# Gate transfer placed behind the convolution, the stage matrix and output weights let in one at a time by GpSimd fills, three x pieces ahead of q's weights, and a new order of the work

## The chip, the core and the metric

The kernel runs on one core of one Trainium2 chip. The metric is the device time in microseconds (us) of one execution; the times below are of separate executions, and the profile is of one more. The engines are TensorE (PE, with its weight loads as PEld), VectorE (DVE), ScalarE (ACT), GpSimd (POOL) and SyncE (SP), each of which works through its own list of instructions in the order written; DMA transfers are issued by SP, POOL and ACT.

## What is computed

From x (2048 x 640), k, v and some weights the kernel makes two results and mixes them row by row:

```
g = sigmoid((x * gate_w).sum(-1))
kv = (4-tap causal filter of k along the rows, per channel) * v
a = x * (fft-convolution of kv with ssm_k along 2048 rows, per channel, + kv * ssm_D)
q, k, v = x @ wqkv, 32 heads of 20; each row attends to rows s, s-2, ..., s-14
b = softmax(q k / sqrt(20)) v, all heads, @ wo
out = g * a + (1 - g) * b
```

## The kernel before

A planner (class `Plan`) runs at build time. The parts of the work are generators (`loads`, `xpose`, `vproj`, `qkproj`, `fragger`, `score_gen`, `pv_gen`, `conv`, `gate`, `h_stream`, ...), each of which asks for one engine at a time with an estimated cost; the planner picks the request whose estimated start plus 120 ns times its priority (table `PRI`) is least, and the instructions are written to the engines' lists in that order. `LEAN_QK`, `LEAN_V` and `LEAN_H` tilt the choice between ACT and DVE for copies out of PSUM; `BG` and `pipe` tell how far the estimated DMA pipe has to be drained before a paced load asks for its fill. The lists are fixed when the kernel runs.

The work in order of time:

- **Projections.** x comes in eight pieces of 256 rows (`xn`). TensorE turns each over (`tx`, 10 transposes a piece), and DVE copies it to `xT`. `psv` (18 units of 10 matmuls, line 528) is the projection to v for one block of 121 rows; it needs the weights `Wv`, which lie in the tile `KX`. `pj` (30 units of 10 matmuls, line 575) is the projection to q and k: for each fifth `ft` of the features first three units of q, then three of k, with the weights `Wqk` (loads W0 for q, W1 for k). Each unit is copied by ACT or DVE to `stg`, of which there are two, one for q and one for k; a new `stg` can be written only when the transfers out of the old one have landed.
- **Fragments.** GpSimd sends the rows of `stg` on to `qb` and `kb` in transfers of up to 20 rows (`fragger`, line 614), three sets of each in turn. Set `t` holds heads 4t to 4t+3.
- **Attention**, for t = 0 to 7: `sc` (line 636) are the scores, ACT takes the exponential (line 643, ten instructions a t), `O` (line 664) is their product with v, and DVE divides (`rd`, `oS`, lines 673 and 676). The four PSUM tiles `ps0` to `ps3` are shared by all stages.
- **Filter of k ("the convolution")** on DVE: 24 multiplications and 18 additions (lines 481 and 488) inside `KX`, from row 64 down, and at the end four products with v (line 492, into `vin`). It starts when the last k load has landed.
- **Gate.** 20 matmuls (`gps`, line 542), an exponential by ACT to `grow`, the first 1024 columns of `KX`, four small DMA transfers on SP's queue from there to `g_nat` (line 551), and three small DVE instructions (lines 554 to 556). The transfers read single rows at a wide stride, and a DVE instruction that writes elsewhere in `KX` behind them waits until they have landed; the transfers in turn wait for the DVE instructions on `KX` ahead of them.
- **Transform** of ssm_k (key h) and kv (key u), each in two halves P of 40 channel groups: per half ten units `s1` (line 697) and eleven `s2` (line 713), each of which ACT or DVE copies out of PSUM. `s2` needs the stage matrix G, four loads into `SX`, which takes the place of `KX`. `Hw` is a copy of the h result with its halves swapped, made by four transfers for each P (lines 805 and 807). 44 products on DVE (line 751), the output projection `op` (line 854, 16 units), the inverse (`i`, lines 820 and 893) and the mix (lines 901 to 908) end the kernel.

SP issues nearly all loads, in the order written. `load` only issues. `paced` first lets GpSimd fill one column of the target, and the load waits for that fill, so that its place in GpSimd's list tells when the load may start. Before, v (8 loads) and ssm_k (16 loads, `h_lin`) are paced.

Of the kernel before, what the change touches and what calls it, by code (L numbers as in the profile page):

```python
# [18 lines left out]
D = 640  # L19
# [26 lines left out]
QC = 160  # L46
CR = 11
WARM = 8
BG = 1491.0


def _np_bf16(a):
# [78 lines left out]
class Req:  # L131


    def __init__(self, engs, cost=0.0, deps=(), take=0, give=(), n=0, move=0.0, pri=None, mode=None, bg=None, mm=0, lean=0.0):
# [3 lines left out]

LAT = {("P", "A"): 230.0, ("P", "D"): 230.0, ("A", "P"): 120.0, ("D", "P"): 120.0, ("A", "D"): 100.0, ("D", "A"): 100.0}
SWITCH = 110.0  # L140
LEAN_QK = -187.0
LEAN_V = -490.0
LEAN_H = 56.0
PRI = dict(loads=0, fragger=0, xpose=-6.6, score_gen=-9.9, pv_gen=-6.9, conv=-3.3, conv_v=-2.7, bulk=0, conv_end=0, qkproj=-6.1, vproj=-6.6,
           gate=-16.1, load_G=0, h_slot=0, p2_slot=41.0, u_slot=0, swaps=0, load_T=0, op_tr=24.4, outproj=37.1, load_q=0, products=28.7, final=-12.8,
           h_stream=(-6.1, 2.1), u_stream=(1.4, 19.9), inverse1=(31.7, 33.5))
PAGE = 256
FETCH = 3600.0

# [1 line left out]
class Plan:  # L151


    def __init__(self, nslots):
        self.at = dict(P=0.0, A=0.0, D=0.0, G=0.0, S=0.0, Q=0.0)
        self.mode = None
        self.count = 0
        self.page = 0.0
        self.pipe = 0.0
        self.row = 0.0  # L160
        lane = []
        self.lane = {"S": lane, "Q": lane, "G": []}
        self.slots = [Bank() for _ in range(nslots)]
        self.streams = []
        self.log = []
# [91 lines left out]
def kernel(  # L257
# [14 lines left out]
    nc = tc.nc  # L272
# [3 lines left out]
    cf = {k: nc.inline_tensor(v, name=f"cf_{k}") for k, v in fft_consts().items()}  # L276
# [32 lines left out]
    Wv, kin, pab, wraw, wl = [KX[:, e - n:e] for e, n in zip(ends, sizes)]  # L309
    grow = KX[:, 0:1024].bitcast(F32)  # L310
    Wv = Wv.rearrange("p (t n) -> p t n", t=NDT)
# [24 lines left out]
    W3 = B_wqkv.rearrange("(t p) (w n) -> p t w n", p=128, w=3)  # L336
# [3 lines left out]
    def ev(name):  # L340
        if name not in E:
            E[name] = Ev()
        return E[name]
# [10 lines left out]
    def load(name, dst, src, us, deps=()):  # L354
        g = yield Req("S", 650.0, deps, move=us)
        nc.sync.dma_start(dst, src)
        mark(name, g)

    def paced(name, dst, src, us):
        g = yield Req("G", 200.0, bg=BG, pri=2)  # L360
        nc.gpsimd.memset(dst[:, 0, 0:1], 0.0)
        yield from load(name, dst, src, us, [g.done])

    def load_x(a):
        yield from load(f"x{a}", xn[:, a], raw(x2, 256 * a * D, [[2 * D, 128], [D, 2], [1, D]]), 1250.0)

    def loads():
        yield from load_x(0)
        yield from load("Wv0", Wv[:, 0:3], W3[:, 0:3, 2, :], 1700.0)
        yield from load_x(1)  # L370
        yield from load("W0", Wqk[:, :, 0, :], W3[:, :, 0, :], 2800.0)
        yield from load_x(2)
        yield from load_x(3)
        yield from load("W1", Wqk[:, :, 1, :], W3[:, :, 1, :], 2800.0)
        for a in range(4, 8):
            yield from load_x(a)
        for c in (1, 0):
            for q in range(4):
                yield from load(f"k{q}{c}", kin[32 * q:32 * q + 32, 3 + 32 * c:35 + 32 * c, :],
                                raw(k2, 32 * c * D + QC * q, [[64 * D, 32], [D, 32], [1, QC]]), 2000.0)  # L380
        for c in range(2):
            for q in range(4):
                yield from paced(f"v{q}{c}", vin[32 * q:32 * q + 32, c], raw(v2, QC * q + 80 * c, [[64 * D, 32], [D, 64], [1, 80]]), 2100.0)
        yield Req("S", 1.0, [ev("xtr")])
        h_lin = p0.tile([128, 80, 2, 64], BF, name="h_lin", tag="HL")
        st["h_lin"] = h_lin
        for P in range(2):
            for q in range(4):
                for c in range(2):
                    yield from paced(f"h{P}{q}{c}", h_lin[32 * q:32 * q + 32, PL * P:PL * P + PL, c, :],  # L390
                                     raw(A_ssm_k, (160 * q + 80 * c + PL * P) * S, [[64, 32], [S, PL], [1, 64]]), 1200.0)
# [12 lines left out]
    def load_G():  # L404
        yield Req("S", 1.0, [ev("conv"), ev("grow"), ev("vproj")])
        SX = p0.tile([128, 10240 + 8192], BF, name="SX", tag="KX")
        st["SX"] = SX
        st[("h", 0)] = SX[:, 0:10240].rearrange("p (c o m l) -> p c o m l", c=2, o=10, m=128)
        G = SX[:, 10240:].rearrange("p (a r b) -> p a r b", a=32, r=2)
        st["G"] = G  # L410
        at("SX", 0.0)
        for a in range(4):
            yield from load(f"G{a}", G[:, 8 * a:8 * a + 8], cf["G"].ap().rearrange("p (a r b) -> p a r b", a=32, r=2)[:, 8 * a:8 * a + 8], 1700.0)

    def load_T():
        yield Req("S", 1.0, [ev("p2")])
        wo = st["p2"].tile([128, NDT, D], BF, name="wo")
        st["wo"] = wo
        yield from load("wo", wo[:], B_wo.rearrange("(t p) n -> p t n", p=128), 2700.0)
        yield Req("S", 1.0, [ev("hw1")])  # L420
        T = st["p2"].tile([128, 64, 2, 32], BF, name="T")
        st["T"] = T
        yield from load("T", st["T"][:], cf["T"].ap().rearrange("p (a r b) -> p a r b", a=64, r=2), 2700.0)
# [112 lines left out]
    def gate():  # L536
        g = yield Req("P", 1300.0, [ev("xtr"), ev("vproj")] + xdeps(0, HS), take=1, mode="g", mm=20)
        gps = psum(g, "gps", (128, 512))
        for dt in range(NDT):
            for c in range(4):  # L540
                o = X0 + HP * (c // 2) + 512 * (c % 2)
                nc.tensor.matmul(gps[32 * c:32 * c + 32, :], lhsT=wgz[:, dt, :], rhs=xT[:, dt, o:o + 512],
                                 start=(dt == 0), stop=(dt == NDT - 1), tile_position=(0, 32 * c), skip_group_check=True)
        mark("gatePE", g)
        r = yield Req("A", 600.0, [g.done], give=g.banks)
        nc.scalar.activation(grow, gps[:], ACT.Exp, scale=-1.0)
        src = grow[0:1, 0:1]
        pt = src.ap[0][0]
        for gg in range(4):
            r = yield Req("S", 500.0, [r.done] if gg == 0 else [], move=200.0)  # L550
            nc.sync.dma_start(g_nat[32 * gg:32 * gg + 32, :], raw(src, 64 * (gg % 2) * pt + 16 * (gg // 2), [[32 * pt, 2], [32, 16], [1, 16]]))
        mark("grow", r)
        r = yield Req("D", 500.0, [Ev(r.done.t + 8000.0)])
        nc.vector.tensor_scalar(g_nat[:], g_nat[:], 1.0, None, ALU.add)
        nc.vector.reciprocal(g_nat[:], g_nat[:])
        nc.vector.tensor_scalar(omg[:], g_nat[:], -1.0, 1.0, ALU.mult, ALU.add)
        mark("gate", r)
# [357 lines left out]
    for gen in (loads, fragger, xpose, score_gen, pv_gen, conv, bulk, conv_v, conv_end, qkproj, vproj, gate, load_G, h_slot, p2_slot,  # L915
                u_slot, swaps, load_T, op_tr, outproj, load_q, products, final):
        plan.add(gen(), PRI[gen.__name__])
    for gen in (h_stream, u_stream, inverse1):
# [33 lines left out]
```

## Time and profile before

| | |
|---|---|
| median of 3 executions | 257.19 us (256.75 to 258.81) |
| profiled execution: time | 257.08 us |
| profiled execution: span | 255.3 us |
| granted TensorE clock, mean | 0.889 of full speed |
| busy: PE, DVE, ACT, POOL | 216.6, 185.5, 168.7, 69.2 us |
| DMA moved | 33.82 MB in 59579 packets, 49212 of them under 512 B |

The span is the time from the first to the last record of the profile, and 1.8 us of the execution lie outside it. No engine is busy all the time, so what bounds the kernel changes from stage to stage, and the views below are read by stage.

### The profile page before, as it was taken

The page shows a single profiled execution, that of the slowest core. Times are in us where ns is not written, and L with a number is a line of the kernel's source. Part 1 is how long each engine was busy: PE and PEld are TensorE (multiplying, and loading weights), DVE is VectorE, ACT ScalarE, POOL GpSimd, SP SyncE. Part 2 cuts the span into 40 slices and gives each one's busy share as a digit, 9 for nine tenths or more (in the row PEclk, how much of TensorE's full clock was granted, in tenths as well). Part 3 has the DMA queues.
Part 4 walks back from the last instruction along what each step waited for, and adds up shares of the span by engine and source line. Part 5 has one row for each costly group of instructions (what it writes and reads, how often), then busy time and mean ns, then how long its engine had stood idle before and what let it go on. Part 6 is the DMA issues. An engine that isn't in the chain of part 4 may idle for free.

```text
span 255.3 us, 8331 instructions
## 1 busy us (share of the span) xinstructions
PE 216.6 (85%) x3648; PEld 168.6 (66%) x3654; DVE 185.5 (73%) x221; ACT 168.7 (66%) x221; POOL 69.2 (27%) x142
## 2 busy tenths in 40 slices
PE   7799999990799799979859898899999999994590
PEld 3699888860456556746636687688887798884350
DVE  1224799942887978979848879989999998053851
ACT  2143455590348857658948969989986589767971
POOL 6698897220153635438500000000000000000000
PEclk9999999996599979999655569989999999999568
DMA  6999958992789888932992002960089992400663
GB/s 231 303 336 183 183 76 151 146 152 31 120 114 161 130 138 140 137 80 52 256 239 90 1 5 53 229 135 3 3 173 218 193 232 78 103 3 5 157 158 103
DMA packets 59579, 33.82 MB, mean 133 GB/s; under 512 B 49212, under 2 KB 56008, under 8 KB 58904
## 3 DMA queue, kind: packets, MB, share of 16 engines
q1 hardware_dynamic: 55192, 27.08, 53.6%
q0 software_dynamic: 3792, 5.81, 11.4%
q8 instruction: 28, 0.46, 0.8%
q10 hardware_dynamic: 560, 0.42, 0.5%
q14 instruction: 7, 0.06, 0.1%
HBM read 20.01 MB, written 2.62 MB: 89 GB/s over the span
## 4 chain that ended last, share of the span: by engine, by line
PE 50%; DVE 17%; DMA 11%; ACT 8%; issue 8%; POOL 2%; SPq 1%; DVEq 0%; POOLq 0%; ACTq 0%
PE psv L528 10%; PE op L854 10%; PE pj L575 9%; DMA kb<-stg 7%; PE i L820 7%; DVE Hs L286 5%; PE s L713 3%; DVE stg L286 3%; ACT ETall L643 3%; PE sc L636 3%; DMA xn<-in_A_q_dram 3%; ACT UC L284 2%; PE O L664 2%; PE tx L467 2%; ACT yb L901 2%
## 5 line engine op out<-in xcount | busy, mean ns | idle before, releaser
L643 ACT ACTIVATE ETall<-sc 121x912 bf16<-121x912 f32 (+1 forms) x80 | 63.4, 856 | 26.1 <-PE sc L636 25.6
L575 PE MATMUL pj<-xT,Wqk 128*128 128x342 bf16 (+1 forms) x300 | 51.5, 322 | 0.4 <-ACT ETall L643 0.4
L575 PEld LDWEIGHTS <-Wqk 128*128 128x128 bf16 x300 | 28.8, 100 | 16.1 <-issue 0.7
L636 PE MATMUL sc<-qb,kb 31*128 31x114 bf16 x576 | 22.5, 239 | 16.1 <-DVE stg L286 8.0
L284 ACT CAST UC<-s 128x960 bf16<-128x960 f32 (+2 forms) x32 | 29.4, 992 | 2.2 <-PE s L713 1.8
L636 PEld LDWEIGHTS <-kb 31*128 31x128 bf16 x576 | 13.4, 103 | 25.9 <-issue 17.4
L481 DVE TENSOR_TENSOR KX<-KX 128x1760 bf16<-128x1760 bf16 (+1 forms) x24 | 27.7, 1162 | 3.0 <-DMA g_nat<-KX 1.7
L614 POOL DMA_DIRECT2D qb<-stg x36 | 18.1, 505 | 39.9 <-PE sc L636 25.6
L528 PE MATMUL psv<-KX,xT 128*121 128x320 bf16 x180 | 28.0, 306 | 0.0
L854 PE MATMUL op<-wo,oT 128*128 128x128 bf16 (+1 forms) x154 | 24.9, 317 | 0.7 <-issue 0.2
L284 ACT CAST VW<-psv 121x640 bf16<-121x640 f32 x16 | 11.1, 695 | 21.0 <-PE psv L528 21.0
L528 PEld LDWEIGHTS <-xT 128*121 128x121 bf16 x180 | 24.2, 138 | 1.1
L488 DVE TENSOR_TENSOR KX<-KX 128x1760 bf16<-128x1760 bf16 (+1 forms) x18 | 18.8, 1042 | 7.2 <-DMA g_nat<-KX 6.9
L713 PEld LDWEIGHTS <-SX 64*128 64x128 bf16 x512 | 19.9, 98 | 3.5 <-issue 2.5
L854 PEld LDWEIGHTS <-oT 128*128 128x128 bf16 x160 | 17.1, 149 | 7.6 <-issue 2.3
L614 POOL DMA_DIRECT2D kb<-stg x36 | 17.9, 503 | 10.1 <-ACT stg L284 6.7
L284 ACT CAST stg<-pj 128x684 bf16<-128x684 f32 (+1 forms) x14 | 10.4, 743 | 14.9 <-PE pj L575 11.3
L286 DVE COPY xT<-tx 128x1280 bf16<-128x1280 bf16 x8 | 6.6, 825 | 18.0 <-PE tx L467 18.0
L286 DVE CAST SX<-s 128x1024 bf16<-128x1024 f32 (+1 forms) x15 | 17.6, 1198 | 2.6 <-PE s L713 1.6
L286 DVE CAST stg<-pj 128x726 bf16<-128x726 f32 (+1 forms) x16 | 14.3, 892 | 6.7 <-DMA kb<-stg 5.2
L858 ACT ACTIVATE bl<-op,omg 128x640 bf16<-128x640 f32 x16 | 12.7, 795 | 9.3 <-PE op L854 9.3
L664 PEld LDWEIGHTS <-ETall 121*128 121x128 bf16 x576 | 16.5, 99 | 3.4 <-issue 1.8
(71 smaller groups left out, 378.6 us busy)
## 6 DMA issues: line engine op xcount, KB each, us to landing
xn<-in_A_q_dram SPq DMA_DIRECT2D x8, 320.0 KB, 9.1
KX<-in_A_k_dram SPq DMA_DIRECT2D x8, 320.0 KB, 9.9
vin<-in_A_v_dram SPq DMA_DIRECT2D x8, 320.0 KB, 7.7
h_lin<-in_A_ssm_k_dram SPq DMA_DIRECT2D x16, 160.0 KB, 4.7
Hw<-SX SPq DMA_DIRECT2D x4, 640.0 KB, 9.5
Hw<-Hs SPq DMA_DIRECT2D x4, 640.0 KB
out_dram<-SX SPq DMA_DIRECT2D x20, 120.0 KB, 2.2
kb<-stg POOLq DMA_DIRECT2D x28, 85.1 KB, 4.7
```

The lines of the kernel that those rows point to most:

```text
L284: nc.scalar.copy(dst, src)
L286: nc.vector.tensor_copy(dst, src)
L481: eng.tensor_tensor(d, kin[:, n + 3 - j:n + 3 - j + m, :], w.to_broadcast([128, m, QC]), ALU.mult)
L488: eng.tensor_tensor(ta if j else dst, ta, tb, ALU.add)
L528: nc.tensor.matmul(ps[0:BK, n0 // 320, 0:320], lhsT=xT[:, dt, s0:s0 + BK], rhs=Wv[:, dt, n0:n1], start=(dt == 0), stop=(dt == NDT - 1))
L575: nc.tensor.matmul(ps[:, i, 0:n], lhsT=Wqk[:, dt, w, 128 * ft:128 * ft + 128], rhs=xT[:, dt, s0:s0 + n], start=(dt == 0), stop=(dt == NDT ...
L614: nc.gpsimd.dma_start(dst[r0:r0 + rows, 0:wd], stg[fa - f0:fb - f0, 0:wd])
L636: nc.tensor.matmul(sc[:, hh, BQ * bb:BQ * bb + BQ], lhsT=kb[r:r + DH + NF, BK * b:BK * b + 128], rhs=qb[r:r + DH + NF, BQ * b:BQ * b + BQ] ...
L643: nc.scalar.activation(ETall[0:BK, e, :, 0:BQ * nb], sc[0:BK, :, 0:BQ * nb], ACT.Exp, scale=SCALE)
L664: nc.tensor.matmul(O[:, (b - b0) // 6, c0:c0 + 21], lhsT=ETall[0:BK, e, hh, BQ * bb:BQ * bb + 128], rhs=VW[0:BK, b, 4 * t + h4, :], start= ...
L713: nc.tensor.matmul(ps[:, c, 160 * jj:160 * jj + 160], lhsT=st["G"][rows, j0 + jj, rr, :], rhs=Am[rows, rr].rearrange("p o (q j) l -> p j ( ...
L854: nc.tensor.matmul(op[:, n0:n1], lhsT=oT[:, ft].rearrange("p h m a -> p a (h m)")[:, t, :], rhs=wo[:, ft, n0:n1], start=(ft == 0), stop=(f ...
```

## The change

Six edits.

1. `loads`: the pieces of x numbered 1, 2 and 3 are issued ahead of the load W0 (q's weights), where W0 stood between pieces 1 and 2, and W1 follows piece 4.
2. `load_G` and `load_T`: the four loads of G and the load of the output weights `wo` become paced.
3. `gate`: the three DVE instructions are asked for only after the convolution has ended.
4. `BG`, the tilts, the table of priorities and the planner's first value of `pipe` get other numbers, which gives a new order on all engines.
5. `paced` gets a flag for tiles with one more dimension.
6. The planner is told 2800 ns instead of 1700 for the load of `Wv`.

```diff
-BG = 1491.0
+BG = 1266.0
...
-PRI = dict(loads=0, fragger=0, xpose=-6.6, score_gen=-9.9, pv_gen=-6.9, conv=-3.3, conv_v=-2.7, bulk=0, conv_end=0, qkproj=-6.1, vproj=-6.6,
+PRI = dict(loads=0, fragger=0, xpose=-9.2, score_gen=-8.6, pv_gen=-5.7, conv=-1.6, conv_v=-24.1, bulk=0, conv_end=0, qkproj=-4.2, vproj=-4.8,
...
-    def paced(name, dst, src, us):
+    def paced(name, dst, src, us, deep=False):
         g = yield Req("G", 200.0, bg=BG, pri=2)
-        nc.gpsimd.memset(dst[:, 0, 0:1], 0.0)
+        nc.gpsimd.memset(dst[:, 0, 0, 0:1] if deep else dst[:, 0, 0:1], 0.0)
         yield from load(name, dst, src, us, [g.done])
...
-        yield from load("Wv0", Wv[:, 0:3], W3[:, 0:3, 2, :], 1700.0)
-        yield from load_x(1)
+        yield from load("Wv0", Wv[:, 0:3], W3[:, 0:3, 2, :], 2800.0)
+        for a in (1, 2, 3):
+            yield from load_x(a)
         yield from load("W0", Wqk[:, :, 0, :], W3[:, :, 0, :], 2800.0)
-        yield from load_x(2)
-        yield from load_x(3)
+        yield from load_x(4)
         yield from load("W1", Wqk[:, :, 1, :], W3[:, :, 1, :], 2800.0)
-        for a in range(4, 8):
+        for a in range(5, 8):
             yield from load_x(a)
...
-            yield from load(f"G{a}", G[:, 8 * a:8 * a + 8], cf["G"].ap().rearrange("p (a r b) -> p a r b", a=32, r=2)[:, 8 * a:8 * a + 8], 1700.0)
+            yield from paced(f"G{a}", G[:, 8 * a:8 * a + 8], cf["G"].ap().rearrange("p (a r b) -> p a r b", a=32, r=2)[:, 8 * a:8 * a + 8], 1700.0, True)
...
-        yield from load("wo", wo[:], B_wo.rearrange("(t p) n -> p t n", p=128), 2700.0)
+        yield from paced("wo", wo[:], B_wo.rearrange("(t p) n -> p t n", p=128), 2700.0)
...
-        r = yield Req("D", 500.0, [Ev(r.done.t + 8000.0)])
+        r = yield Req("D", 500.0, [Ev(r.done.t + 5000.0), ev("conv")])
```

SyncE's list, from the third transfer on and around the gate (`xn` is x, `KX` with the weights is Wv, `Wqk` is W0 and then W1; `KX` from A_k is k, `vin` v, `h_lin` ssm_k, `SX` from cf_G the stage matrix; a line with - is before, one with + after):

```order
 L356 DMA xn<-in_A_q_dram 128x1280
 L356 DMA KX<-in_B_wqkv_dram 128x3x640
+L356 DMA xn<-in_A_q_dram 128x1280 x3
+L356 DMA Wqk<-in_B_wqkv_dram 128x5x640
 L356 DMA xn<-in_A_q_dram 128x1280
 L356 DMA Wqk<-in_B_wqkv_dram 128x5x640
```

Pieces 1, 2 and 3 now stand ahead of the first `Wqk` load. Further down the same list:

```order
-L356 DMA vin<-in_A_v_dram 32x64x80 x5
+L356 DMA vin<-in_A_v_dram 32x64x80 x8
+L356 DMA h_lin<-in_A_ssm_k_dram 32x40x64 x12
 L551 DMA g_nat<-KX 32x1x16 x4
-L356 DMA vin<-in_A_v_dram 32x64x80 x3
-L356 DMA h_lin<-in_A_ssm_k_dram 32x40x64 x16
+L356 DMA h_lin<-in_A_ssm_k_dram 32x40x64 x4
 L356 DMA SX<-cf_G 128x2048 x4
```

The gate's four transfers stood behind the fifth v load, and stand now behind all v loads and twelve of the sixteen of ssm_k.

VectorE's list around the gate before, in the middle of the convolution (DMAHW4 and DMAHW6 are the counters of the gate's second and last transfer, DMAHW3 and DMAHW5 of the others; DMASW are fragments):

```order
L488 TENSOR_TENSOR KX<-KX 128x1760 [waits DMAHW4_49,DVE_49]
L481 TENSOR_TENSOR KX<-KX 128x1760 [waits DMAHW6_49,DVE_49]
L286 CAST stg<-pj 128x2x363 [waits DMASW4_49,DMASW3_49,DMASW5_49,DMASW2_49,DMASW6_49,DMASW1_49,DMASW7_49,PE_49,Activation_49]
L481 TENSOR_TENSOR KX<-KX 128x1760
L673 RECIPROCAL rd_84<-O 114x48 [waits PE_49]
```

and after, behind the convolution's last instructions (here DMAHW2 to DMAHW5 are the gate's four transfers):

```order
L492 TENSOR_TENSOR vin<-KX,vin 128x2560
L286 CAST stg<-pj 128x2x363 [waits DMASW3_49,DMASW2_49,DMASW5_49,DMASW1_49,DMASW6_49,DMASW0_49,DMASW7_49,PE_49,Activation_49]
L286 CAST stg<-pj 128x2x363 [waits PE_49]
L554 TENSOR_SCALAR g_nat<-g_nat 128x16 [waits DMAHW4_49,DMAHW5_49,DMAHW3_49,DMAHW2_49]
L555 RECIPROCAL g_nat<-g_nat 128x16 [waits DVE_49]
L556 TENSOR_SCALAR omg<-g_nat 128x16 [waits DVE_49]
L286 CAST stg<-pj 128x2x363 [waits PE_49]
```

No instruction of the convolution waits for a transfer of the gate any more; the gate's second transfer waits for the convolution's last addition instead, and the last three copies of the projections to `stg` stand behind the four products (line 492).

GpSimd's list at its end (`qb` and `kb` are fragments, `SX` and `wo` the new fills, line 763 adds ssm_D to `h_lin` and waits for ssm_k's loads):

```order
+L361 MEMSET h_lin 32x1 x3
+L361 MEMSET SX 128x1 x2
 L614 DMA qb_80<-stg 20x2052 x4
 L614 DMA kb_77<-stg 8x2178
 L614 DMA kb_77<-stg 20x2178 x2
-L614 DMA kb_79<-stg 20x2178 x4
+L614 DMA kb_79<-stg 20x2178
+L361 MEMSET SX 128x1
+L763 TENSOR_TENSOR h_lin<-h_lin,Dz 128x80
+L614 DMA kb_79<-stg 20x2178 x3
+L361 MEMSET SX 128x1
+L361 MEMSET wo 128x1
```

The fills of G stand among the last fragments, two ahead of them and two between or behind them, and the fill of `wo` is last; the first fill of `SX` waits for the end of the convolution and for the gate's transfers.

TensorE does the same 3648 matmuls. Ahead of the first scores stood 8 `tx`, 17 `psv` and 9 `pj` units, and stand now 8, 14 and 8, in which one `psv` comes between the first and second `tx`; ahead of t = 1 all 18 `psv` and 15 `pj` stand in both. The gate's matmuls stood among the scores of t = 0 and stand now just ahead of t = 4, and of the `pj` 12 instead of 11 lie between the first scores of t = 1 and of t = 4.

## Rows read from the trace of the kernel before

**Rows 1.** Busy time by stretch: us, PE, PEld, DVE, ACT, POOL, PEclk, DMA share, GB/s.

```profile
9.20:49.80 40.60, 40.60 (x323) 35.21 (x320) 27.59 (x26) 17.80 (x25) 32.01 (x48) 1.00 1.04 200
...
57.40:65.40 8.00, 0.04 (x2) 0.06 (x1) 3.02 (x4) 0.00 (x0) 0.00 (x0) 0.59 0.43 64
...
76.10:111.20 35.10, 31.08 (x541) 20.70 (x542) 29.76 (x41) 24.64 (x32) 16.53 (x46) 0.95 0.92 140
...
129.10:132.70 3.60, 1.08 (x9) 0.42 (x8) 1.59 (x2) 1.51 (x2) 0.00 (x0) 0.50 1.03 236
...
153.30:193.00 39.70, 36.28 (x771) 31.84 (x772) 38.29 (x37) 37.06 (x43) 0.00 (x0) 0.96 0.47 101
```

**Rows 2.** Who waited for whom: us in total, times, longest us.

```profile
DVE KX L488 <- DMA g_nat<-KX: 6.9, 1, 6.9
```

**Rows 3.** Timeline, 50 to 77 us: start, us, engine, line, operation, [idle before <-releaser].

```profile
52.14 1.26 PE L542 MATMUL gps<-xT,wgz 128*32 128x512 bf16 x20
...
65.40 0.49 PE L636 MATMUL sc<-qb,kb 31*128 31x114 bf16 x12 [7.96 <-DVE stg L286]
...
65.82 3.10 PE L575 MATMUL pj<-xT,Wqk 128*128 128x349 bf16 x10
...
76.08 0.38 PE L636 MATMUL sc<-qb,kb 31*128 31x114 bf16 x7 [0.38 <-DMA kb<-stg]
```

**Rows 4.** Timeline of the first 10 us.

```profile
6.77 0.82 DVE L286 COPY xT<-tx 128x1280 bf16<-128x1280 bf16 x1 [4.97 <-PE tx L467]
...
9.23 5.14 PE L528 MATMUL psv<-KX,xT 128*121 128x320 bf16 x30
```

**Rows 5.** The chain that ended last, in order of time: start, us, what.

```profile
14.37 0.56 PE tx L467 x10
14.93 1.36 PE psv L528 x10
...
38.64 1.49 PE pj L575 x10
...
57.93 2.66 DMA g_nat<-KX
```

**Rows 6.** Timeline, 35 to 50 us.

```profile
35.92 3.50 POOL L614 DMA_DIRECT2D qb<-stg  x7 [0.20 <-issue]
...
41.23 3.46 POOL L614 DMA_DIRECT2D kb<-stg  x7 [1.54 <-ACT stg L284]
...
49.85 0.41 PE L636 MATMUL sc<-qb,kb 31*128 31x114 bf16 x16
```

**Rows 7.** Fragments qb issued from 35.9 to 38.9 us: issue to landing.

```profile
DMA to landing us min/median/max: 2.2/2.7/3.0
```

**Rows 8.** Fragments kb issued from 41.2 to 44.2 us: issue to landing.

```profile
DMA to landing us min/median/max: 3.8/6.4/6.6
```

**Rows 9.** Fragments kb issued from 72.1 to 75.1 us: issue to landing.

```profile
DMA to landing us min/median/max: 2.4/3.4/3.4
```

**Rows 10.** Timeline, 108 to 134 us.

```profile
118.46 1.48 DVE L492 TENSOR_TENSOR vin<-KX,vin 128x2560 bf16<-128x2560 bf16 x1
...
120.01 1.85 SPq L356 DMA_DIRECT2D SX<-cf_G  x4
...
122.68 2.96 POOL L614 DMA_DIRECT2D kb<-stg  x6 [1.38 <-DVE stg L286]
...
131.81 0.27 PE L636 MATMUL sc<-qb,kb 31*128 31x114 bf16 x1 [1.84 <-DMA kb<-stg]
```

**Rows 11.** Fragments kb issued from 122.7 to 126.2 us: issue to landing.

```profile
DMA to landing us min/median/max: 6.7/9.8/10.8
```

**Rows 12.** Timeline, 156 to 161 us: first and last issue of the first swap.

```profile
156.80 0.55 SPq L805 DMA_DIRECT2D Hw<-SX  x1
...
160.48 2.36 SPq L807 DMA_DIRECT2D Hw<-SX  x1
```

**Rows 13.** The page, part 6: the swap's transfers, KB each, us to landing.

```profile
Hw<-SX SPq DMA_DIRECT2D x4, 640.0 KB, 9.5
```

More of the change, by code (lines that the diff above doesn't have):

```diff
@@ L140 @@
 SWITCH = 110.0
-LEAN_QK = -187.0
-LEAN_V = -490.0
-LEAN_H = 56.0
-PRI = dict(loads=0, fragger=0, xpose=-6.6, score_gen=-9.9, pv_gen=-6.9, conv=-3.3, conv_v=-2.7, bulk=0, conv_end=0, qkproj=-6.1, vproj=-6.6,
-           gate=-16.1, load_G=0, h_slot=0, p2_slot=41.0, u_slot=0, swaps=0, load_T=0, op_tr=24.4, outproj=37.1, load_q=0, products=28.7, final=-12.8,
-           h_stream=(-6.1, 2.1), u_stream=(1.4, 19.9), inverse1=(31.7, 33.5))
+LEAN_QK = -248.0
+LEAN_V = 87.0
+LEAN_H = -137.0
+PRI = dict(loads=0, fragger=0, xpose=-9.2, score_gen=-8.6, pv_gen=-5.7, conv=-1.6, conv_v=-24.1, bulk=0, conv_end=0, qkproj=-4.2, vproj=-4.8,
+           gate=-0.8, load_G=0, h_slot=0, p2_slot=10.2, u_slot=0, swaps=0, load_T=0, op_tr=4.7, outproj=37.5, load_q=0, products=6.3, final=-18.6,
+           h_stream=(-3.7, -4.9), u_stream=(0.9, 2.5), inverse1=(33.7, 30.7))
 PAGE = 256
@@ L158, in __init__ @@
         self.page = 0.0
-        self.pipe = 0.0
+        self.pipe = 2000.0
         self.row = 0.0
```

## Prediction

> **What bounds the kernel now.** I read the busy times by stretch first [rows 1]. From 9.2 to 49.8 us TensorE is busy without a gap (40.60 of 40.60): the projections bound the start. From 57.4 to 65.4 it does nothing (0.04 of 8.00), ACT nothing, GpSimd nothing, and VectorE works 3.02. From 76.1 to 111.2, the attention of t = 1 to 3 with the convolution beside it, TensorE is busy 31.08 and VectorE 29.76 of 35.10: neither has much room, and each waits for the other. From 129.1 to 132.7 TensorE works 1.08 of 3.60. From 153.3 to 193.0 ACT (37.06) and VectorE (38.29) copy without pause, and behind that the order is fixed by products and inverse.
>
> The waits name the cause of the first hole [rows 2]: the convolution's addition stood 6.9 us behind a gate transfer. The timeline shows what hung on it [rows 3]: behind the held VectorE stood a copy to `stg`, its `pj` kept a PSUM tile, and the next scores came 7.96 us late, at 65.40. The unit after the hole took 3.10 us where one takes 1.49 [rows 5]; the stretch was granted 0.59 of the clock [rows 1], which lies between the levels 1.2 and 2.4 GHz. The second hole is the scores of t = 6 waiting for a `kb` fragment [rows 10]: it was issued from 122.68 on, right behind four loads of G from 120.01, and such fragments took 9.8 us to land [rows 11], where those of the quiet stretch at 72 us took 3.4 [rows 9].
>
> **The change part by part**, against the profiled execution (span 255.3, time 257.08; the median of the three others, 257.19, is the same within 0.1 us).
>
> *The start.* The first `psv` ran at 9.23, behind the transposes of two pieces; now it follows those of piece 0, whose copy ended at 6.77 + 0.82 = 7.59 [rows 4]. It also needs `Wv`, whose landing no row shows; it was issued ahead of piece 1. Bounds: start at 7.6 (-1.6) or 9.2 (0). I take 8.0, **-1.2**, nearer to the copy. W0 is later by two pieces. Piece 1 had landed ahead of 9.2; two more pieces and W0 are 1.47 MB, 7.4 us at the 200 GB/s of [rows 1], so W0 is there by 16.6, ahead of its first unit behind five `psv` and four `tx`, at 8 + 5 x 1.36 + 4 x 0.56 = 17.0: 0.
>
> *First scores.* Ahead of them now lie 7 more `tx`, 14 `psv` and 8 `pj`: 7 x 0.56 + 14 x 1.36 + 8 x 1.49 = 34.9 [rows 5]. The same sum on the old order from 9.23 (6, 17 and 9) is 39.9 and ends at 49.1, and the scores ran at 49.85 [rows 6], so 0.7 goes to changeovers: now 8.0 + 34.9 + 0.6 = 43.5. The fragments: GpSimd ends q's seven at 39.42 as before; k's were issued at 41.23, 1.1 behind the end of their last unit [rows 5, 6], and that unit now ends some 2 us sooner (8.0 + 7 x 0.56 + 12 x 1.36 + 6 x 1.49 + 0.6 = 37.8), so k's follow at 39.4 and the fourth, the last of set 0, at 40.9. With 2.7 us to land [rows 7] it is there at 43.6, with 6.6 [rows 8] at 47.5: a wait of 0.1 to 4.0. The 6.6 fell beside v loads, which now start only behind these fragments; I take 1.0.
>
> *t = 1.* Behind the last k unit of set 1 TensorE has three more units, 4.5 us; 1.1 to the issue, 0.5 for a second issue and 3.4 to land [rows 9] make 5.0. Wait 0.5, up to 3.7 with 6.6 to land [rows 8]; 0.38 was there before [rows 3]. I take +0.5. The gate's matmuls leave the stretch: -1.26 [rows 3]. The hole goes, -8.0, and the slow unit behind it, 3.10 - 1.49 = 1.6 less. Sum to the start of t = 1: -1.2 + 1.0 + 0.5 - 1.3 - 8.0 - 1.6 = **-10.6**, so 65.5 instead of 76.1. VectorE keeps up: its conv instructions begin when k has landed, as before, and it gains the 6.9 us that it stood [rows 2].
>
> *t = 1 to 3.* The stretch has one `pj` more (1.49) and the gate's matmuls (1.26), and TensorE had 4.0 us free there [rows 1]; VectorE's list has one tap more and one `stg` copy less. From 0 to +2.7; I take +0.5, since the row has room. Start of t = 4: **-10.1**, at 101.1.
>
> *t = 4.* VectorE now does the four products, 4 x 1.48 = 5.9 us [rows 10], before it takes the last three units out of PSUM; before, copies stood between the products. Two or three of the four PSUM tiles are held meanwhile, and scores and exponentials share the rest. From 0 to three products, +4.4; I take **+1.5**. The copies feed sets 6 and 7, which are wanted a whole t later.
>
> *Gate.* Its transfers wait on SP for the last addition, then take 4 issues of about 0.5 and 2.66 [rows 5], 4.7 us; VectorE's instruction that needs them stands behind four products and two copies, over 7 us: 0. If twelve ssm_k loads on SP hold them up, the copy behind that instruction is late, and with it k's last fragments: see the rivals. Queued behind the waiting transfer on SP are four ssm_k loads, G and `wo`; G could not start earlier anyway, as its place is the convolution's.
>
> *Fills.* GpSimd's first fill of `SX` waits for the products; queued behind it are q's fragments of set 7 and k's last ones. k's wait for the last `stg` copy in any case, which is later than the fill, and set 7 is wanted 17 us on: 0. Two G loads instead of four and `wo` then run beside the `kb` fragments of set 6. Their landing lies between 3.4 and 9.8; with 6.6 or less the wait of t = 6 is gone: 3.60 - 1.08 = **-2.5**, at worst 0.
>
> *Second half.* From 153.3 to 193.0 there were 30 `s1`, 41 `s2` and 5 `tr` units, 0.52 us each [rows 1]; now 26, 44 and 5. But h's second half is begun early, and the first half ends 30 units (15.7 us) into this stretch; the first product on VectorE stands some 24 units later, 12.5 us. The swap between needs 3.7 us of issues and 9.5 to land [rows 12, 13], 13.2. **+0.5**, from 0 to +4.
>
> Sum: -10.1 + 1.5 - 2.5 + 0.5 = -10.6. Span 244.7, time **246.5 us**. With every part at its good end t = 1 starts 12.6 earlier, and with -2.5 at t = 6 the time is 242.0.
>
> **The rivals.**
>
> 1. *Fragments late.* Six v loads are now let in at one place, at 43 us, and G, v and ssm_k all run beside fragments. If set 0 and set 1 need 6.6 us as in [rows 8], the waits are 4.0 and 3.7 instead of 1.5: 252.7. For it: the DMA share of 0.92 in t = 1 to 3 [rows 1]. Against: the v fills stand behind k's fragments. The Trainium skill, DMA: Bandwidth & Descriptors, section Queues, rings and completion order, says that each DMA engine takes turns between the queues that have work, so that six loads waiting in SP's queue would cost a GpSimd fragment no more than one. By that rule 6.6 is the ceiling here; the 9.8 beside G and `wo` speaks against so firm a ceiling.
>
> 2. *The fills change nothing at t = 6*: the first two G loads do the harm. 249.0.
>
> 3. *The hole moves.* The change does not do what it says: the gate's transfers come late, and VectorE stands before the last copy, so that the 8.0 and 1.6 us come back at t = 4 to 6. 246.5 + 9.6 = 256.1. For it: SP's list has twelve paced loads ahead. Against: the last of those fills stands among t = 3's fragments.
>
> 4. *Slower: the clock.* After the hole a unit took 3.10 us. If TensorE's shorter waits at the first scores and at t = 1 leave it at the low level through t = 1 to 3, each of the 12 `pj` costs 1.61 more, 19.3 less the 1.3 us still free: 264.5. From seven slow units on the gain is eaten. Against: the stretch was granted 0.95 with the same units [rows 1]. [...]
>
> 5. *The second half waits for the swap* or for products in the new order: +4 instead of +0.5, 250.0.
>
> **How the numbers follow.** Chances: forecast 0.52 (alone 242 to 249), fragments late 0.13, fills without effect 0.13, hole moved 0.09, slower by the clock 0.05, second half 0.08. The likeliest is 246.5. Rival 3 and rival 4 hold 0.14 and stay outside; the range reaches from the good ends, 242.0, to the first rival, 253.0. One per cent, 2.6 us, is about what a measurement of this kernel can tell. Faster than 254.5: forecast and rivals 1, 2 and 5, all but 0.01, 0.85; rival 3 lies within 1% and with the rest makes 0.09; slower 0.06, rival 4 and a worse rival 3.
>
> **What would show it.** The wait of the convolution for `g_nat` is gone, and no stretch before t = 1 has TensorE still for more than 4 us. First `psv` near 8.0, first scores near 44.5, t = 1 near 65.5, t = 4 near 101. `kb` of set 6 lands within 7 us and t = 6 starts without a wait. The last attention output ends near 142 instead of 153.3, and from there to the end it is 102 us as before. Wrong: a new hole of over 5 us on TensorE between 43 and 140, a low granted clock in t = 1 to 3, or a first product on VectorE that waits for the swap.

## The result, and the profile after

The changed kernel takes 248.98 us (median of 4, 247.85 to 251.77) against 258.0 before in the same series (4 runs): ratio 0.964, interval 0.957 to 0.971. The forecast was 246.5, from 242.0 to 253.0. The profiled execution took 247.85 with a span of 246.1. Some executions run 1.5% or more above the fastest of their kernel; the ratios leave them out, and the profiles of e3, e5, e10 and e12 are of such executions.

Where the time went, by the start of each stage in the two profiled executions (a t by its first scores; for the first of all, t = 1 and t = 4 the part behind the wait that cut them, where one did):

| stage | before | forecast | after | gained in the stage: forecast, measured |
|---|---|---|---|---|
| first `psv` | 9.23 | 8.0 | 7.26 | 1.2, 2.0 |
| first scores | 49.85 | 44.5 | 44.40 | 4.2, 3.5 |
| t = 1 | 76.08 | 65.5 | 66.39 | 5.2, 4.2 |
| t = 4 | 111.25 | 101.1 | 101.73 | -0.5, -0.2 |
| t = 5 | 120.52 | | 110.69 | -1.5, 0.3 |
| t = 6 | 129.10 | | 119.54 | 0, -0.3 |
| t = 7 | 140.93 | | 128.39 | 2.5, 3.0 |
| end of attention | 153.26 | 142 | 140.02 | 0, 0.7 |
| output projection | 192.96 | | 183.49 | -0.5, -3.8 |
| end of the span | 255.3 | 244.7 | 246.1 | 0, -0.3 |

Each gain stands in the row of the start that it changes. The stretches of the changed kernel, to be read beside [rows 1]: busy time by stretch, with the columns given there.

```profile
53.50:64.50 11.00, 11.00 (x100) 7.33 (x94) 10.76 (x14) 4.57 (x7) 6.71 (x15) 1.00 0.99 154
66.40:101.70 35.30, 32.67 (x563) 21.50 (x563) 31.56 (x41) 25.77 (x33) 16.79 (x44) 0.95 0.83 130
140.00:183.50 43.50, 37.57 (x789) 32.84 (x787) 39.61 (x39) 35.08 (x41) 0.00 (x0) 0.94 0.57 123
```

Where TensorE worked 0.04 of 8.00 us before, it is now busy for all of the 11 us ahead of t = 1. The attention of t = 1 to 3 has the same length (35.3 and 35.1) and the same clock (0.95). The second half takes 43.5 us where it took 39.7.

The timeline of the changed kernel, TensorE at the starts of the table (compare [rows 3, 4, 6, 10]):

```profile
7.26 1.54 PE L528 MATMUL psv<-KX,xT 128*121 128x320 bf16 x10 [1.01 <-DVE xT L286]
...
42.75 0.67 PE L636 MATMUL sc<-qb,kb 31*128 31x114 bf16 x8
43.67 0.22 PE L636 MATMUL sc<-qb,kb 31*128 31x114 bf16 x1 [0.25 <-DMA kb<-stg]
44.40 0.38 PE L636 MATMUL sc<-qb,kb 31*128 31x114 bf16 x7 [0.50 <-DMA kb<-stg]
...
65.75 0.22 PE L636 MATMUL sc<-qb,kb 31*128 31x114 bf16 x1 [0.83 <-DMA kb<-stg]
66.39 0.38 PE L636 MATMUL sc<-qb,kb 31*128 31x114 bf16 x7 [0.43 <-DMA kb<-stg]
...
119.54 1.20 PE L636 MATMUL sc<-qb,kb 31*128 31x114 bf16 x16 [0.34 <-ACT ETall L643]
```

The waits for fragments are 0.75 us at the first scores and 1.26 at t = 1; at t = 6 only 0.34 us is left, and that for ACT. The same timeline, VectorE and SP around the gate, the loads of G and the first swap (`g_nat` is the gate, `SX` G, `Hw` the swap, line 751 the first product):

```profile
98.63 5.98 DVE L492 TENSOR_TENSOR vin<-KX,vin 128x2560 bf16<-128x2560 bf16 x4
99.46 2.42 SPq L551 DMA_DIRECT2D g_nat<-KX  x4
106.79 0.17 DVE L554 TENSOR_SCALAR g_nat<-g_nat 128x16 f32<-128x16 f32 x1
107.64 9.44 SPq L356 DMA_DIRECT2D SX<-cf_G  x4
...
154.72 0.54 SPq L805 DMA_DIRECT2D Hw<-SX  x1
...
158.38 2.38 SPq L807 DMA_DIRECT2D Hw<-SX  x1
...
163.35 4.60 DVE L286 CAST UC<-s 128x1024 bf16<-128x1024 f32 x4
166.31 0.46 SPq L805 DMA_DIRECT2D Hw<-Hs  x1
...
170.68 0.66 DVE L751 TENSOR_TENSOR SX<-UC,SX 128x960 bf16<-128x960 bf16 x1 [2.73 <-DMA Hw<-SX]
...
172.52 2.05 PE L713 MATMUL s<-UC,SX 64*128 64x160 bf16 x32 [1.88 <-DVE oT L286]
```

The gate costs nothing: its transfers are issued in 2.42 us beside the products, and line 554 runs without a wait. The new wait is the last group: VectorE, through with its copies at 167.95, stands 2.73 us for the swap, and TensorE then 1.88 for the copy behind the product. Before, the swap was issued 3.5 us behind the last attention output [rows 12]; now it is 14.7 us behind.

The landing of the `kb` fragments of set 6, issued from 112.1 to 116.1 (compare [rows 11]):

```profile
DMA to landing us min/median/max: 4.7/4.8/6.4
```

### The profile page after: what moved, and what is told of

Read it like the earlier page. It is cut to its first block, busy times and chain, and to the rows that moved or that the text cites. A ratio compares the mean times of both kernels' runs of the same rounds, so it can differ in the third digit from the quotient of the medians.

```text
span 246.1 us, 8342 instructions
## 1 busy us (share of the span) xinstructions
PE 215.8 (88%) x3654; PEld 167.2 (68%) x3654; DVE 185.8 (76%) x220; ACT 168.6 (69%) x222; POOL 68.8 (28%) x147
## 4 chain that ended last, share of the span: by engine, by line
PE 49%; DMA 13%; POOL 13%; issue 9%; ACT 9%; DVE 4%; SPq 1%; ACTq 0%; POOLq 0%; DVEq 0%
PE op L854 10%; PE pj L575 9%; PE i L820 7%; PE O L664 6%; DMA Hw<-SX 5%; PE sc L636 5%; ACT ETall L643 4%; PE s L713 4%; DMA kb<-stg 3%; POOL qb L614 3%; DMA mm<-ca_mm 3%; DMA KX<-in_A_k_dram 3%; PE psv L528 2%; POOL kb L427 2%; POOL qb L428 2%
## 5 line engine op out<-in xcount | busy, mean ns | idle before, releaser
L643 ACT ACTIVATE ETall<-sc 121x912 bf16<-121x912 f32 (+1 forms) x80 | 63.4, 855 | 12.5 <-PE sc L636 11.6
L575 PE MATMUL pj<-xT,Wqk 128*128 128x342 bf16 (+1 forms) x300 | 49.0, 314 | 1.0 <-ACT ETall L643 0.6
L528 PE MATMUL psv<-KX,xT 128*121 128x320 bf16 x180 | 27.3, 300 | 1.0 <-DVE xT L286 1.0
L636 PE MATMUL sc<-qb,kb 31*128 31x114 bf16 x576 | 23.4, 241 | 5.4 <-ACT ETall L643 2.0
L284 ACT CAST UC<-s 128x960 bf16<-128x960 f32 (+2 forms) x25 | 22.3, 971 | 7.9 <-PE s L713 6.7
L854 PE MATMUL op<-wo,oT 128*128 128x512 bf16 (+1 forms) x160 | 25.7, 322 | 0.0
L528 PEld LDWEIGHTS <-xT 128*121 128x121 bf16 x180 | 23.4, 134 | 2.2 <-issue 1.2
L284 ACT CAST stg<-pj 128x684 bf16<-128x684 f32 (+1 forms) x17 | 12.5, 746 | 14.9 <-PE pj L575 9.2
L284 ACT CAST VW<-psv 121x640 bf16<-121x640 f32 x15 | 10.4, 696 | 17.8 <-PE psv L528 17.8
L286 DVE CAST UC<-s 128x1024 bf16<-128x1024 f32 (+1 forms) x17 | 19.5, 1195 | 0.0
L858 ACT ACTIVATE bl<-op,omg 128x640 bf16<-128x640 f32 x16 | 12.7, 794 | 8.6 <-PE op L854 8.6
L820 PE MATMUL i<-F,Hw 128*128 128x128 bf16 x160 | 18.3, 219 | 0.0
```

Of the source, the lines that this page charges most:

```text
L284: nc.scalar.copy(dst, src)
L286: nc.vector.tensor_copy(dst, src)
L528: nc.tensor.matmul(ps[0:BK, n0 // 320, 0:320], lhsT=xT[:, dt, s0:s0 + BK], rhs=Wv[:, dt, n0:n1], start=(dt == 0), stop=(dt == NDT - 1))
L575: nc.tensor.matmul(ps[:, i, 0:n], lhsT=Wqk[:, dt, w, 128 * ft:128 * ft + 128], rhs=xT[:, dt, s0:s0 + n], start=(dt == 0), stop=(dt == NDT ...
L636: nc.tensor.matmul(sc[:, hh, BQ * bb:BQ * bb + BQ], lhsT=kb[r:r + DH + NF, BK * b:BK * b + 128], rhs=qb[r:r + DH + NF, BQ * b:BQ * b + BQ] ...
L643: nc.scalar.activation(ETall[0:BK, e, :, 0:BQ * nb], sc[0:BK, :, 0:BQ * nb], ACT.Exp, scale=SCALE)
```

## The experiments

All compare with the kernel before on the same chip, whose median was 258.5 (e1 to e4, 14 runs), 258.7 (e5 to e8, 13 runs) and 258.7 (e9 to e12, 11 runs). Every edit makes the planner write a new order from some point on; how far the order is still the same is said where it matters.

**e1: edit 3 alone.**

```diff
-        r = yield Req("D", 500.0, [Ev(r.done.t + 8000.0)])
+        r = yield Req("D", 500.0, [Ev(r.done.t + 5000.0), ev("conv")])
```

> The kernel before, with the gate's three VectorE instructions asked for only behind the convolution (edit 3) and nothing else. Theory A (order): VectorE's instructions behind the gate's transfers still write the tile from which these read, so the convolution's addition still waits 6 to 7 us for the gate transfer and TensorE still stands about 8 us before the scores of t = 0 are done; time within 1% of before, 255 to 260. Rival B (the edit itself frees VectorE): the wait is gone and the time is about 247 to 249.

262.73 us, ratio 1.016 (1.007 to 1.026). The hole is as it was; waits, and the timeline of TensorE, of e1:

```profile
DVE KX L488 <- DMA g_nat<-KX: 6.2, 1, 6.2
```

```profile
65.20 0.49 PE L636 MATMUL sc<-qb,kb 31*128 31x114 bf16 x12 [7.36 <-DVE stg L286]
65.62 3.10 PE L575 MATMUL pj<-xT,Wqk 128*128 128x349 bf16 x10
```

Theory A holds on the wait: the edit that names the convolution does not free it. Its time, 255 to 260, is missed: a loss of 1.6% comes later, in the new order (t = 4, counted here and below from its very first scores, took 14.4 us instead of 11.5); it was not followed further.

**e2: the false wait alone.** The order on TensorE, VectorE, ACT and GpSimd is that of before; each of the eight transfers names the one row that it reads.

```diff
-            nc.sync.dma_start(g_nat[32 * gg:32 * gg + 32, :], raw(src, 64 * (gg % 2) * pt + 16 * (gg // 2), [[32 * pt, 2], [32, 16], [1, 16]]))
+            _ = [nc.sync.dma_start(g_nat[32 * gg + 16 * k:32 * gg + 16 * k + 16, :], grow[64 * (gg % 2) + 32 * k:64 * (gg % 2) + 32 * k + 1, :].rearrange("p (m h n) -> p m h n", h=2, n=16)[:, :, gg // 2, :]) for k in range(2)]
```

> The kernel before in its own order on TensorE, VectorE, ACT and GpSimd; only the gate's four transfers are written as eight, each of which names the one row that it reads, so that no instruction of the convolution waits for them any more. Theory A: the stop of VectorE (6.9 us) is the whole cause of TensorE's hole of 8.0 us and of the slow unit behind it (1.6 us): scores of t = 1 at 66 to 68 instead of 76.1, and the time 246 to 250, unless the 9 us are partly given back at t = 4 to 6. Rival C (something else is late behind it, the copies to stg or the fragments): t = 1 at 72 or later, time 253 to 257.

254.6 us, ratio 0.987 (0.979 to 0.994). The scores of t = 1 run at 66.10, 10 us earlier, as theory A has it, but t = 2 starts at 82.22, only 3.1 us earlier, and the span ends 1.3 us earlier. The timeline of e2 shows the hole again, behind t = 1:

```profile
66.10 0.86 PE L636 MATMUL sc<-qb,kb 31*128 31x114 bf16 x16
...
74.01 0.91 DVE L286 CAST stg<-pj 128x726 bf16<-128x726 f32 x1 [5.89 <-DMA qb<-stg]
74.97 0.59 PE L636 MATMUL sc<-qb,kb 31*128 31x114 bf16 x16 [4.48 <-DVE stg L286]
75.50 3.10 PE L575 MATMUL pj<-xT,Wqk 128*128 128x349 bf16 x10
```

VectorE now waits to overwrite `stg` until q's fragments have landed, 6.3 us behind their issue, beside the last three v loads and the first of ssm_k; TensorE stands 4.48 us and its next unit takes 3.10 us. A stop in t = 4 grows as well, from 1.80 us to 3.06, and the unit behind it takes 3.03. Of the 9.6 us of my sum the old order passes on 3 or 4 (3.9 by the medians): rival C by the time, with its place one stage later than it said.

**e3: the gate's priority alone.**

```diff
-           gate=-16.1, load_G=0, h_slot=0, p2_slot=41.0, u_slot=0, swaps=0, load_T=0, op_tr=24.4, outproj=37.1, load_q=0, products=28.7, final=-12.8,
+           gate=-0.8, load_G=0, h_slot=0, p2_slot=41.0, u_slot=0, swaps=0, load_T=0, op_tr=24.4, outproj=37.1, load_q=0, products=28.7, final=-12.8,
```

> The kernel before with one number of the table of priorities changed, the gate's from -16.1 to -0.8. In its order the gate's matmuls stand behind all scores of t = 0 and its transfers behind most of the convolution; one addition still waits for them. Theory A: the hole of 8 us before t = 1 is gone, scores of t = 1 at 66 to 69; a wait of VectorE for the gate's transfer of up to 5 us may be left in t = 1 to 3; time 247 to 254. Rival B (it was edit 3 that freed VectorE): hole and time as before, 255 to 260.

258.62 us (10 runs), ratio 0.998 (0.993 to 1.003). The hole is gone and t = 1 runs at 64.87 and 68.1, so it is the place of the gate and not edit 3 that removes it. But t = 2 took 17.4 us (79.69 to 97.06, six `pj` units in it instead of three) where it took 12.3, and nearly all of the gain went there: t = 3 starts at 97.06, against 97.67 before. A wait for the gate's transfer of 1.9 us is left. Theory A was right on the hole and wrong on the time.

**e4: the changed kernel with the gate early.**

```diff
-           gate=-0.8, load_G=0, h_slot=0, p2_slot=10.2, u_slot=0, swaps=0, load_T=0, op_tr=4.7, outproj=37.5, load_q=0, products=6.3, final=-18.6,
+           gate=-16.1, load_G=0, h_slot=0, p2_slot=10.2, u_slot=0, swaps=0, load_T=0, op_tr=4.7, outproj=37.5, load_q=0, products=6.3, final=-18.6,
```

> The changed kernel with the gate's priority back at -16.1 and edit 3 kept, which puts the gate's matmuls back among the scores of t = 0 and two instructions of the convolution behind its transfers. Theory A: VectorE waits 4 to 7 us for the gate's transfer, TensorE stands up to 8 us before t = 1, and the time is 253 to 258, most of the gain gone. Rival B (edit 3 suffices): no wait, 247 to 251.

253.88 us, ratio 0.977 (0.967 to 0.987), 4 to 5 us above the changed kernel. The false wait is back, but short: 2.85 and 0.66 us of VectorE; SP issued the gate's transfers in 4.55 us, where it took 7.90 before. t = 1 was at 67.76 (66.39), t = 4 at 105.5 (101.73). In the new order the gate's place is worth 4 to 5 us, between the two theories.

**e5: fills of G and wo taken out of the changed kernel.** TensorE's order is the same to the last scores of t = 7.

```diff
-            yield from paced(f"G{a}", G[:, 8 * a:8 * a + 8], cf["G"].ap().rearrange("p (a r b) -> p a r b", a=32, r=2)[:, 8 * a:8 * a + 8], 1700.0, True)
+            yield from load(f"G{a}", G[:, 8 * a:8 * a + 8], cf["G"].ap().rearrange("p (a r b) -> p a r b", a=32, r=2)[:, 8 * a:8 * a + 8], 1700.0)
...
-        yield from paced("wo", wo[:], B_wo.rearrange("(t p) n -> p t n", p=128), 2700.0)
+        yield from load("wo", wo[:], B_wo.rearrange("(t p) n -> p t n", p=128), 2700.0)
```

> The changed kernel with the four loads of G and the load of wo let in at once again, as before (edit 2 undone); TensorE's order is the same up to the last scores of t = 7. Theory A: the five transfers start together at about 105 to 107 and the kb fragments of set 6, issued from 110 on, land after 8 us or more instead of 4.8, so that t = 6 waits 2 to 3 us; last attention output 142 to 143, time 2 to 4 us above the changed kernel, 250 to 253. Rival B (in the new order the G loads come early enough anyhow): no wait at t = 6, time within 1 us of the changed kernel.

255.52 us (250.99 to 258.12), ratio 0.978 (0.968 to 0.988). The wait at t = 6 did not come back: the four loads went out together at 111.83, 7.4 us ahead of the fragments, and these landed in

```profile
DMA to landing us min/median/max: 5.3/5.7/6.0
```

So that wait stays away without the fills, and rival B holds for t = 6, though not for the time (within 1 us). The profiled execution was already 5 us late at t = 1, where its order does not differ; TensorE had stood 1.55 us at 43 us and two `psv` then took 2.92 and 2.63 us instead of 1.5. Whether the fills are worth anything behind t = 7, where the order does differ, stays open.

**e6: the changed kernel with the old order of the first loads.**

```diff
-        for a in (1, 2, 3):
-            yield from load_x(a)
+        yield from load_x(1)
         yield from load("W0", Wqk[:, :, 0, :], W3[:, :, 0, :], 2800.0)
-        yield from load_x(4)
+        yield from load_x(2)
+        yield from load_x(3)
...
```

> The changed kernel with the loads of x, W0 and W1 in their order of before (and the planner's 1700 ns for Wv). Theory A: the first psv falls back to about 9.2 from 7.26, the first scores from 42.75 to 45 or later, and the time rises by 1 to 2 us, 249 to 251, if the order behind it is as good. Rival B (the first psv waits for Wv or for the copy in either case): first psv within 0.5 us, time within 1 us. As the planner makes a new order for all that follows, the start is to be read from the trace and the total only with care.

257.18 us (10 runs), ratio 0.995 (0.991 to 1.000). The first `psv` is at 8.70, 1.4 us later than in the changed kernel. At the first scores nothing of it is seen: they start at 44.34 with nine `pj` ahead of them, and at 42.75 with eight in the changed kernel, and one `pj` is 1.45 us. In five profiled executions with the changed kernel's order up to there (after, e5, e7, e11, e12) TensorE is through with these units at anything from 42.4 to 44.1, so what the start itself is worth is not shown. The 8 us come from the order that follows: v's fills stand two, three and three instead of six together, and the same hole as in e2 opens in t = 1 (2.04 us for a `stg` copy, then units of 3.10, 2.60 and 2.85 us). t = 1 to 3 took 41.2 us at a clock of 0.83, where the changed kernel took 35.3 at 0.95.

**e7: ssm_k's second half behind its first.** The order is the same to the scores of t = 7.

```diff
-           h_stream=(-3.7, -4.9), u_stream=(0.9, 2.5), inverse1=(33.7, 30.7))
+           h_stream=(-3.7, 2.1), u_stream=(0.9, 2.5), inverse1=(33.7, 30.7))
```

> The changed kernel with one number changed: the priority of ssm_k's second half from -4.9 to 2.1, its value of before. Its second half no longer begins among the scores of t = 6 and 7; TensorE, VectorE and ACT first finish the first half. Theory A (the 3.8 us that the second half of the kernel lost come from the first swap, issued 14.7 us behind the last attention output instead of 3.5): the swap is issued within 6 us of the last attention output, the first product does not wait for it, the stretch from there to the output projection is about 40 us instead of 43.5, and the time 244 to 247. Rival B (the copies of ACT and VectorE, the same in sum, set that stretch): product without a wait, but 43 us, time within 1 us of the changed kernel.

247.56 us, ratio 0.958 (0.950 to 0.965). The swap is issued 5.7 us behind the last attention output and the first product does not wait. Busy time by stretch of e7, t = 1 to 3 and the second half:

```profile
66.40:104.65 38.25, 35.39 (x566) 22.58 (x566) 31.47 (x42) 25.69 (x33) 16.50 (x44) 0.87 0.81 120
142.60:183.70 41.10, 36.74 (x794) 31.81 (x788) 38.58 (x37) 36.85 (x42) 0.00 (x0) 0.98 0.52 113
```

The second half takes 41.1 us instead of 43.5: theory A. Much of it was lost ahead of it, in the same order as the changed kernel's, by the clock (first row; counted from the start of t = 1 behind its wait, 67.07, it is 37.6 us at 0.86).

**e8: e2 with edit 3, and v's fills behind set 0.**

```diff
-        g = yield Req("G", 200.0, bg=BG, pri=2)
+        g = yield Req("G", 200.0, [ev("set0")] if name[0] == "v" else [], bg=None if name[:2] in ("v0", "v1", "v2") or name in ("v30",) else BG, pri=2)
...
-        r = yield Req("D", 500.0, [Ev(r.done.t + 8000.0)])
+        r = yield Req("D", 500.0, [Ev(r.done.t + 5000.0), ev("conv")])
```

> The kernel before with the gate's transfers by single rows (as in e2), its VectorE instructions behind the convolution (edit 3), and the fills of seven v loads asked for as soon as set 0 of the fragments is sent, so that they stand behind k's first seven fragments, as six do in the changed kernel. In e2 the hole came back at 69 to 75, where VectorE waited 5.9 us for q's fragments, which landed in 6.3 us beside three v loads and the first of ssm_k. Theory A (what the new order adds to the gate's move is that v's loads are over before t = 1): no wait of VectorE for a fragment over 3 us before t = 2, t = 2 at 76 to 78, time 249 to 252. Rival C (with the hole gone VectorE and TensorE are simply full there): t = 2 at 80 or later, time 253 to 256.

254.42 us, ratio 0.985 (0.975 to 0.995), no better than e2. From t = 1 to t = 2 it took 12.2 us instead of e2's 16.1, and VectorE waited no more than 2.4 us for a fragment, as theory A has it; but t = 2 starts at 80.39, as rival C has it. Then TensorE stood 3.89 us in t = 4 for a `kb` fragment, and t = 4 took 15.4 us where it took 11.5. Early v loads make that hole smaller, and another opens; the time is rival C's.

**e9: the four products first, in the kernel before.** The order is the same up to t = 4.

```diff
-PRI = dict(loads=0, fragger=0, xpose=-6.6, score_gen=-9.9, pv_gen=-6.9, conv=-3.3, conv_v=-2.7, bulk=0, conv_end=0, qkproj=-6.1, vproj=-6.6,
+PRI = dict(loads=0, fragger=0, xpose=-6.6, score_gen=-9.9, pv_gen=-6.9, conv=-3.3, conv_v=-24.1, bulk=0, conv_end=0, qkproj=-6.1, vproj=-6.6,
```

> The kernel before with one number changed, the priority of the four products from -2.7 to -24.1, its value in the changed kernel; the order is that of before up to t = 4. VectorE then does the four products in a row, ahead of four copies to stg; the loads of G and wo are not paced, but may start as soon as the products are done. In e5, without the fills, the wait at t = 6 did not come back, and G had been issued 5 to 7 us ahead of the kb fragments of set 6 instead of 2.7. Theory D (the products' place took the wait away): no wait over 0.5 us for kb at t = 6, and the time 254 to 256, 2 to 3 us below before. Rival A (the fills did): the kb fragments of set 6 land after 8 us or more again, t = 6 waits 2 to 4 us, time 256 to 260.

264.86 us, ratio 1.027 (1.019 to 1.035). The fragments of set 6 landed in 5.0 us instead of 9.8, with G issued 18 us ahead of them; yet t = 6 waited:

```profile
139.03 0.56 PE L636 MATMUL sc<-qb,kb 31*128 31x114 bf16 x7 [2.09 <-DMA kb<-stg]
```

With the copies to `stg` behind the products, three `pj` units moved from t = 4 into t = 5, and t = 4 and t = 5 took 12.8 and 12.7 us instead of 11.5 and 8.6; the fragments then went out only 2 us ahead of their scores. Neither theory holds: a short landing doesn't help where the issue is late.

**e10: the new numbers in the old code**, and none of the other edits.

```diff
-BG = 1491.0
+BG = 1266.0
...
-           gate=-16.1, load_G=0, h_slot=0, p2_slot=41.0, u_slot=0, swaps=0, load_T=0, op_tr=24.4, outproj=37.1, load_q=0, products=28.7, final=-12.8,
+           gate=-0.8, load_G=0, h_slot=0, p2_slot=10.2, u_slot=0, swaps=0, load_T=0, op_tr=4.7, outproj=37.5, load_q=0, products=6.3, final=-18.6,
...
-        self.pipe = 0.0
+        self.pipe = 2000.0
```

> The kernel before with all numbers of the changed one (BG, tilts, priorities, the first value of pipe) and none of its other edits: old order of the first loads, G and wo not paced, gate without its new dependence. In its order the gate's matmuls stand behind t = 0, one addition still waits for the gate's transfers, and v's fills stand two, three and three. Theory (the new order carries the gain before t = 4): no hole of over 4 us before t = 1, t = 4 at 102 to 105, time 249 to 253. Rival (the order is worth little without the edits): 254 to 258.

260.37 us (254.2 to 264.1, too scattered for a ratio). The large hole is gone (t = 1 at 68.1), but t = 1 has e6's (2.79 us, then units of 3.10 and 2.91), t = 4 starts at 112.3, later than before, and nothing was gained. The theory fails: the new numbers do not carry the gain without the edits, with which they also give another order.

**e11 and e12: the changed kernel and e7 again, side by side.**

> The changed kernel once more, beside the next on the same chip: 247 to 250, and in its trace a first product that waits 2 to 3 us for the swap and 43 to 44 us from the last attention output to the output projection.

> The kernel of e7 once more, on the same chip as the changed kernel. If the swap's place is worth what e7's trace showed (41.1 us instead of 43.5 from the last attention output to the output projection), its time is 1.5 to 3 us below that of the changed kernel; if ACT and VectorE set the end in any case, within 1 us of it.

248.30 us, ratio 0.967 (0.960 to 0.973), and 246.83 us, ratio 0.951 (0.943 to 0.958), six runs each. In e11 the product waited 2.88 us and the second half took 43.5; in e12 there was no wait and 41.3. The version with one number changed is faster by 1.5 us in the medians, and the intervals of the two ratios do not meet, though single times overlap (247.0 to 251.1 and 243.8 to 249.0). It is the fastest of this study.

## Why the prediction was right, point by point

- **The hole.** -9.6 was right for the changed kernel: no hole ahead of t = 1, no slow unit. The cause is shown by e2 (the false wait gone in the old order, hole gone) and by e1 and e3 (it is the gate's place, a number of the table, and not edit 3). What the sum took for granted failed outside it: that the 9.6 us arrive at the end. In the old order only 3 or 4 do, as rival 3 foresaw but at other places, above all t = 1, where `stg` waits for fragments. Why the changed kernel keeps them is not shown: e4, e6, e8 and e10 each lack a part, and each is some 4 us or more above it, but each also has an order of its own, so they do not tell which edit is needed.
- **Start and first scores.** 7.26 is right behind the first copy, which ended at 6.29 + 0.82, so the lower bound was the right end; how much of this arrives later stays open (e6). The scores were whole at 44.40 against 44.5: fragments landed in 3.0 us, near the low end.
- **t = 1 and t = 1 to 3.** 66.39 and 35.3 us against 65.5 and 35.6. The wait was 1.26 instead of 0.5, as set 1 took 4.5 us to land, not 3.4. Rival 1 did not come. The Trainium skill, DMA: Bandwidth & Descriptors, section Queues, rings and completion order, has each DMA engine take turns between the queues that have work; the ceiling of 6.6 us was my own reading of it. The 4.5 us stay below it, but k's fragments in e2 took up to 7.9 beside v loads: 6.6 is no ceiling.
- **t = 4** was mis-sized: +1.5 forecast, -0.3 measured. The sum left out that t = 4 now has three `pj` units where it had four, 1.6 us less; with that its +1.5 becomes -0.1. In e9 the products in a row went with a t = 4 that was 1.4 us longer though it had three units fewer.
- **t = 6**: right size (-2.5 and -3.0), wrong cause. The step on the fills fails in e5, so that the size came right by luck. What differs from before is that two of the four loads of G go out from 107.64 on, 4.5 us ahead of the `kb` fragments, and the others behind fills beside them, where all four went out 2.7 us ahead; in e5 it was all four, 7.4 us ahead. The fragments themselves go out 7.4 us ahead of the scores instead of 6.4. Which piece of the order does that is open; the products' place alone is not it (e9).
- **Second half**: the term that failed, +0.5 forecast and +3.8 measured, which is rival 5; a first product that waits for the swap is also one of the signs of being wrong that the prediction named. The swap started where I had it, 14.7 us into the stretch (15.7), and VectorE came to the product 13.2 us later (12.5). But the last part of the swap landed 16.0 us behind the first issue, not 13.2. Most of this miss could be read in the trace of before: 9.5 us is the median of four parts, and the product waits for the last. The landing of the last two parts before, issued at 158.04 and 160.48:

```profile
DMA to landing us min/median/max: 11.3/11.4/11.5
```

With 11.3 us for the last part the swap of before took 3.7 + 11.3 = 15.0 us, and no other swap was near it. So the second swap, issued from 166.31 on, can stand for 1.0 us at most. The wait of 2.73 us and TensorE's of 1.88 behind it follow; e7 and e12 take the early start away, and with it the wait and 2.3 us. The other 1.5 us of the 3.8 are left in both (41.1 and 41.3 us against 39.7), and no run shows why.

- **The clock** (rival 4): 0.95 in t = 1 to 3 as hoped, and again in e11, but not safe. e5, e7 and e12, in the same order there, were granted 0.86 and took 37.6 or 37.7 us. The Trainium skill, TensorE: Matmul & The Clock Gate, section HAM oscillation, tells of a kernel whose wait for a load was longer than the matmuls of its round, and which began every round at the low clock. That is not this stretch: its stops, of about 1 us, are shorter than the work between them, and slow units followed some of them only.

The profiled time, 247.85, is 1.35 above the forecast: 0.9 up to t = 1 and 3.3 in the second half were missing, and t = 4, t = 6 and t = 7 gave 3.0 more than the sum had. That the total came this near is in part luck: these errors offset each other. Two figures of the prediction do not come out of its own terms: the good ends up to t = 1 add up to 12.4 us, not 12.6, and once the 1.3 us still free are taken off it takes eight slow units, not seven, to eat the gain.

## What to carry to other kernels

Price a removed wait by what the next resource allows, not by its length: e2 took away 9.6 us and kept 3 or 4, because behind the late engine stood transfers that its lateness had been hiding. Where a planner writes the order, an edit is worth what the order that follows makes of it (e6: 1.4 us at its own place, none of it seen at the first scores, 8 at the end), so test edits in the order in which they will run. Before work is begun early to fill gaps, ask which transfer starts only when the older half of it is done.

## What was not expected of the hardware

- The same order and nearly the same stop gave different clocks. At 79 to 80 us the changed kernel's TensorE stood 1.06 and 0.36 us and one `pj` then took 2.44 us; in e7 it stood 0.90 and 0.28 us and two took 3.0 each, against 1.6 at the full clock. That makes 2.3 us in t = 1 to 3 between two kernels that do not differ up to there. In e11 it was one unit of 2.44 again, in e5 and e12 two of 3.0; why stays open.
- Eight transfers of one row each took SP 8.23 us to issue in e2, and four strided ones took 7.90 before, behind the same five v loads; where they stood behind other work (the changed kernel) four took 2.42. Of the long times 3.23 and 3.44 us went to the first transfer alone, which took 0.66 in the changed kernel. So the number of transfers does not set the time; what does is not shown (in e4, behind five v loads again, four took 4.55).
